# Talking-heads attention with a gated MLP: weight conversions and operand splits spread over three products, and another pool order

## The chip, the cores and the metric

The kernel runs on one core of one Trainium2 chip. The metric is the device time of one execution in microseconds (us). Of the five engines the text names PE (TensorE; PEld is its weight load, which runs beside its matmuls), DVE (VectorE), ACT (ScalarE), POOL (GpSimd) and SP (SyncE, here only a queue that issues transfers, in order). Each engine works through its own list of instructions in the order of that list, and an instruction that has to wait holds up those behind it.

## The reference

The reference computes attention in which the heads are mixed before and after the softmax, and then a gated MLP on its result, all in fp32:

```python
scores = scale * np.matmul(q, k.transpose(0, 1, 3, 2))        # q, k, v: 4 x 12 x 448 x 64
scores = np.einsum('bhij,hg->bgij', scores, w_pre)            # w_pre, w_post: 12 x 12
attn = np.exp(scores - np.max(scores, axis=-1, keepdims=True))
attn = attn / (np.sum(attn, axis=-1, keepdims=True) + 1e-09)
attn = np.einsum('bhij,hg->bgij', attn, w_post)
x = np.matmul(attn, v).transpose(0, 2, 1, 3).reshape(B * S, H * D)   # 1792 x 768
g = x @ w_gate                                                # w_gate, w_val: 768 x 1536
return (g * (1.0 / (1.0 + np.exp(-g))) * (x @ w_val)) @ w_out  # w_out: 1536 x 768
```

The weights of the MLP arrive as 64-bit floats, two 32-bit words each.

## The kernel before

**Attention** takes the first 400 us, batch after batch; the change leaves it as it is. It leaves X of the last two batches (896 tokens) in the on-chip memory as a high and a low part, and seven sums and blocks of X of the first two batches in device memory.

**Weights.** A weight is handled in 36 units of 128 x 768 elements: 12 of w_gate and 12 of w_val (indices 0 to 23, in turn), 12 of w_out (24 to 35). `load_raw` (L641) fetches the raw words; `convert` turns them into fp32 in seven operations: ACT's abs (L658), POOL's clamp (L660; on DVE for the first three units), and five on DVE (L662, L664, L668, L670, L672). `keep` (L675) stores the result to `w_d` in device memory, from where later products fetch it. A product with fp32 exactness takes each operand as a high part `hi`, made by ACT, and a low part `lo`, made by DVE as the difference, and issues hi*hi, lo*hi and hi*lo.

**Three products** follow on PE:

1. the gate and value products of the 896 tokens on chip: for each of 12 column blocks f four products of 18 matmuls (L810, L811, L814), upg and upv for two halves of 448 tokens. ACT takes the silu (L819), DVE the product with the value (L827). Units 0 to 23 are converted just before they are used, and split (`whi` L692, `wlo` L688). Beside that run the first w_out units, and `x_load` (L711) and `x_split` (L719 on ACT, L717 on DVE) of the seven X operands of the next product.
2. the same for the other 896 tokens as a Strassen-Winograd scheme: per f seven products of half size (`product`, L755, L756, L758), whose weights are combined (`w_sums`, L726 to L730) and split (L740 ACT, L737 DVE) first, and whose results are combined after (`combine`: copies a, b, c, d by ACT at L767, sums by DVE at L770, the silus sg0 and sg1 by ACT at L773, the products m0 and m1 by DVE at L780). Copy b frees the accumulator y for the seventh product. Results go to device memory or are summed (`a_sum`, L796, and `a_keep`, stores of L788). Six w_out units are converted beside it.
3. the product with w_out, again as seven terms of the same scheme (`AO`, index i), each of seven blocks c of 128 rows (`block`, 18 matmuls of L897, L898, L899). Each block needs a row tile `ar` (L876, and L872 where two are added), split into `ah` (L890, ACT) and `al` (L882, DVE); each term needs three units `o_b` (L857) or sums of them `ot` (`t_load` L845, `t_sum` L849), split into `ohi` (L867) and `olo` (L863). The first three row tiles of term 0 stand in an older tile, `a_first`.

**What sets the order.** Each step is registered with a number, `at_ff(n, fn)`, and the steps are issued in order of these numbers; one unit of n is about 1.1 us of the first product (48 products of 3.4 units in 184 us). `span` (163.2) is where the second product starts and `DOWN` where the third does. A unit that is wanted at n has d = n - 0.9, and these steps:

```python
d = n - LEAD
n1 = END + (d - 24.5) / 1.8                          # load_raw
for step, x in enumerate((17.2, 16.8, 12.9, 12.4, 11.9, 11.4, 10.9, 10.0)):
    at_ff(d - x, later(convert, u, step))            # 0: ACT, 1: POOL, 2 to 7: DVE
at_ff(d - 8.9, later(keep, u))
if u[0] != "o":
    at_ff(d - 3.8, later(split_w, b, u, False))      # whi, ACT
    at_ff(d - 2.8, later(split_w, b, u, True))       # wlo, DVE
```

**Pools.** At `DOWN` the pools of the second product on the right side of the on-chip memory (`t_p` temporaries, `mt` products, `xq` X operands, `ss` weight sums) are closed and those of the third take their place from the same end on, in the order in which they are opened: `ar` (six row tiles) first. A tile of a new pool waits for the last readers of what lay in its address range. `mag`, the tile of steps 0 to 7, has two buffers, and so unit k waits for L672 of the unit two before it in the order of conversions.

## Time and profile before

| | |
|---|---|
| median of 3 runs | 912.32 us |
| lowest and highest | 911.26 and 915.63 us |
| the profiled execution | 909.12 us |
| its span, first to last instruction | 907.4 us |
| mean granted clock of PE | 0.981 |
| busy: PE, PEld, DVE, ACT, POOL | 859.2, 705.9, 650.6, 457.8, 177.3 us |
| DMA | 218.03 MB, mean 240 GB/s |

Times in the trace count from the first instruction of the span. The granted clock is a share of PE's full 2.4 GHz. In waits, "A <- B" means that A stood idle until B had ended. Busy shares are averages over stages that have different limits, so the rows below are cut by stage.

### The profile page before, as it was taken

How to read it: one execution, taken by the hardware profiler on the slowest of the kernel's cores; microseconds unless marked ns; L12 is line 12 of the kernel's file. 1: busy time of each engine (PE TensorE's matmuls, PEld its weight loads, DVE VectorE, ACT ScalarE, POOL GpSimd, SP SyncE). 2: the span in 40 equal slices, each digit the busy share in tenths (PEclk: the TensorE clock that was granted, in tenths of full speed). 3: DMA queues.
4: the chain of work that ended last, by engine and by line, in shares of the span. 5: the costliest groups of instructions: out<-in, count | busy, mean ns of one | idle time of the engine just before them, and what ended most of it. 6: DMA issues, size and time to landing. Idle time of an engine off the chain costs nothing.

```text
span 907.4 us, 26549 instructions
## 1 busy us (share of the span) xinstructions
PE 859.2 (95%) x10886; PEld 705.9 (78%) x10886; DVE 650.6 (72%) x1204; ACT 457.8 (50%) x1042; POOL 177.3 (20%) x257
## 2 busy tenths in 40 slices
PE   8679999898999998989999999999999998999998
PEld 5355676566656666679889889999988998999998
DVE  4466576666756765667999898678988976855853
ACT  3376677666666767744333333255455454344321
POOL 2111111121211111124545543111111011002010
PEclk9698999999989999999999999999999999999999
DMA  9898988998898778536776865537776459968696
GB/s 215 291 323 260 289 284 243 335 305 284 266 321 266 261 232 299 186 108 208 261 254 213 280 224 194 169 105 219 224 224 208 144 199 332 348 212 195 169 303 158
DMA packets 187537, 218.03 MB, mean 240 GB/s; under 512 B 58360, under 2 KB 155160, under 8 KB 187416
## 3 DMA queue, kind: packets, MB, share of 16 engines
q1 hardware_dynamic: 181448, 207.97, 71.3%
q0 software_dynamic: 2080, 5.51, 3.5%
q10 hardware_dynamic: 3888, 2.86, 1.2%
q8 instruction: 86, 1.41, 0.6%
q14 instruction: 35, 0.29, 0.1%
HBM read 136.77 MB, written 79.54 MB: 238 GB/s over the span
## 4 chain that ended last, share of the span: by engine, by line
PE 69%; DVE 12%; DMA 8%; ACT 4%; issue 4%; SPq 2%; POOL 1%; ACTq 0%; DVEq 0%; POOLq 0%
PE pre L324 8%; PE av L410 8%; PE post L368 6%; PE p L755 5%; PE p L758 5%; PE p L756 5%; PE qk L275 5%; PE q L899 5%; PE q L898 5%; PE q L897 5%; DMA rs<-s_all 3%; PE upv L811 2%; PE upv L814 2%; PE upv L810 2%; DVE st L335 2%
## 5 line engine op out<-in xcount | busy, mean ns | idle before, releaser
L341 ACT ACTIVATE e<-pre,st 128x448 f32<-128x448 f32 x180 | 112.5, 630 | 89.6 <-DVE st L335 89.2
L660 POOL TENSOR_SCALAR mag<-mag 128x768 f32<-128x768 f32 x33 | 101.5, 3074 | 258.5 <-ACT mag L658 207.5
L335 DVE TENSOR_REDUCE st<-pre 128x1 f32<-128x448 f32 x180 | 104.3, 619 | 58.2 <-PE pre L324 55.3
L324 PE MATMUL pre<-rs,w_pre_blocks 64*64 64x448 f32 (+1 forms) x720 | 108.0, 573 | 17.7 <-DMA rs<-s_all 11.3
L368 PEld LDWEIGHTS post<-rw,e 60*64 60x64 f32 x5040 | 98.8, 137 | 31.6 <-issue 23.4
L352 POOL TENSOR_SCALAR rw<-w_post_gs,st 128x60 f32<-128x60 f32 x180 | 55.1, 320 | 322.1 <-DVE st L349 240.8
L368 PE MATMUL post<-rw,e 60*64 60x60 f32 x5040 | 105.1, 223 | 5.8 <-issue 4.1
L383 ACT ACTIVATE attnT<-post 128x420 f32<-128x420 f32 (+1 forms) x192 | 91.1, 542 | 22.2 <-PE post L368 21.5
L899 PE MATMUL q<-ohi,al 128*128 128x384 f32 x276 | 93.9, 340 | 2.3 <-DVE al L882 2.3
L897 PE MATMUL q<-ohi,ah 128*128 128x384 f32 x276 | 93.8, 340 | 1.6 <-ACT ah L890 1.6
L275 PE MATMUL qk<-kk,qt 64*64 64x448 f32 x672 | 93.8, 547 | 0.3 <-DVE w_post_gs L148 0.3
L898 PE MATMUL q<-olo,ah 128*128 128x384 f32 x276 | 93.4, 338 | 0.0
L410 PE MATMUL av<-attnT,vn 128*64 128x120 f32 (+9 forms) x1728 | 89.5, 263 | 3.3 <-DVE qt L252 1.8
L410 PEld LDWEIGHTS av<-attnT,vn 128*64 128x64 f32 (+1 forms) x1728 | 70.8, 136 | 16.0 <-issue 5.5
L284 DVE COPY stg<-qk 128x448 f32<-128x448 f32 x120 | 71.0, 617 | 8.3 <-PE qk L275 4.8
L890 ACT ACTIVATE ah<-ar 128x768 fp32r<-128x768 f32 x46 | 38.6, 844 | 58.4 <-PE q L898 28.8
L882 DVE TENSOR_TENSOR al<-ar,ah 128x768 fp32r<-128x768 f32 x46 | 43.8, 953 | 24.3 <-ACT ah L890 24.3
L275 PEld LDWEIGHTS qk<-kk,qt 64*64 64x64 f32 x672 | 32.3, 134 | 34.0 <-issue 22.3
L811 PE MATMUL upv<-x,wlo 128*128 128x448 f32 x144 | 53.2, 369 | 3.9 <-DVE wlo L688 3.7
L658 ACT ACTIVATE mag<-raw 128x768 f32<-128x768 f32 x36 | 32.8, 910 | 45.0 <-DVE w L672 25.4
L899 PEld LDWEIGHTS q<-ohi,al 128*128 128x128 f32 x276 | 52.3, 189 | 3.6 <-DVE al L882 3.6
L897 PEld LDWEIGHTS q<-ohi,ah 128*128 128x128 f32 x276 | 52.4, 190 | 2.5 <-ACT ah L890 2.5
(142 smaller groups left out, 1687.9 us busy)
## 6 DMA issues: line engine op xcount, KB each, us to landing
rs<-s_all SPq DMA_DIRECT2D x88, 448.0 KB, 5.5
s_all<-stg SPq DMA_DIRECT2D x60, 448.0 KB, 4.8
w_d<-w SPq DMA_DIRECT2D x36, 384.0 KB, 4.2
raw<-in_moe_w_gate_dram SPq DMA_DIRECT2D x12, 768.0 KB, 5.9
raw<-in_moe_w_val_dram SPq DMA_DIRECT2D x12, 768.0 KB, 7.4
raw<-in_moe_w_out_dram SPq DMA_DIRECT2D x12, 768.0 KB, 6.0
w<-w_d SPq DMA_DIRECT2D x24, 384.0 KB, 4.8
s_all<-stg SPq DMA_DIRECT2D x39, 224.0 KB, 5.0
```

Of the source, the lines that this page charges most:

```text
L275: nc.tensor.matmul(pt[x][i * HB:(i + 1) * HB], qt[b, c][hs, p, r:r + HB], kk[b, p][hs], start=True, stop=True)
L324: nc.tensor.matmul(pt[r][x * HB:(x + 1) * HB], wpre[i], xs[i, x], start=True, stop=True)
L335: nc.vector.tensor_reduce(sts[b, u][:, 0, r:r + 1], pts[b, t], axis=AX.X, op=ALU.max, negate=True)
L341: nc.scalar.activation(e, pts.pop((b, t)), AF.Exp, bias=st[:, 0, r:r + 1], scale=1.0, accum_out=st[:, 1, r:r + 1])
L368: nc.tensor.matmul(ats[b, u][y][o * HB:(o + 1) * HB, to, :m], et[b, t][i, c * P + x * HB:c * P + (x + 1) * HB], rw[b, t][i, :, :m], start= ...
L383: nc.scalar.activation(attnT[:part, i, n0:n1, y * HS:y * HS + m], pt[:part, n0:n1, :m], AF.Copy)
L410: nc.tensor.matmul(o, vn[b][part, h, c], a, start=(c == 0 and x == 0), stop=(c == NC - 1 and x == 2 - m))
L660: eng.tensor_scalar(mag, mag, f32_of(0x38000000), f32_of(0x47EFFFFF), op0=ALU.max, op1=ALU.min)
L811: nc.tensor.matmul(pt, lo[:, c], xh[:, c, ts], start=False, stop=False)
L897: nc.tensor.matmul(pt, ahi, bhi, start=f == 0, stop=False)
L898: nc.tensor.matmul(pt, ahi, blo, start=False, stop=False)
L899: nc.tensor.matmul(pt, alo, bhi, start=False, stop=f == NFH - 1)
```

## The change

It moves five things in the table of steps, and swaps pools:

- the seven X operands are loaded and split from n = 22 on in steps of 20, not from 14 in steps of 19;
- silu sg0 of the second product goes from 3.4 to 5.15, behind copy b at 5.05;
- the last `a_sum` goes from 8 steps of the last f to DOWN + 4 and DOWN + 6.5, the last `a_keep` from DOWN + 8 to DOWN + 11; `t_load` and `t_sum` go later by 4 to 12;
- three w_out units instead of four are converted in the first product, six in the second as before, and three instead of two in the third;
- raw load, ACT's abs and POOL's clamp come 1.6 sooner for every unit with d over 40;
- `bs` (the splits olo and ohi of odd terms) is opened ahead of `ar`.

```diff
-                n = 14.0 + 19.0 * i
+                n = 22.0 + 20.0 * i
...
-                    (1.05, "a"), (2.05, "c"), (3.1, "c11"), (3.4, "sg0"), (4.05, "d"), (5.05, "b"), (6.1, "c12"), (6.4, "sg1"),
+                    (1.05, "a"), (2.05, "c"), (3.1, "c11"), (5.15, "sg0"), (4.05, "d"), (5.05, "b"), (6.1, "c12"), (6.4, "sg1"),
...
-                    step(8.0, a_sum, f - NFH, 0)
-                    step(8.3, a_sum, f - NFH, 1)
-                    if f < NFC - 1:
-                        step(8.4, a_keep, f - NFH)
-                    else:
-                        at_ff(DOWN + 8.0, later(a_keep, f - NFH))
+                    last = f == NFC - 1
+                    for x, y, fn, *a in ((8.0, 4.0, a_sum, f - NFH, 0), (8.3, 6.5, a_sum, f - NFH, 1), (8.4, 11.0, a_keep, f - NFH)):
+                        at_ff(DOWN + y if last else n + x * T_P, later(fn, *a))
...
-                    at_ff(DOWN + (11, 11.5, 21, 22)[x] + 0.2 * j, later(t_load, bq, j))
-            for i, x in enumerate((20, 29, 33, 40)):
+                    at_ff(DOWN + (17, 17.5, 32, 33)[x] + 0.2 * j, later(t_load, bq, j))
+            for i, x in enumerate((24, 37, 41, 45)):
...
-            if ku < 4:
-                n = (2.75 + 2 * ku) * T_F[0]
-            elif ku < 10:
-                n = span + 10 + 22 * (ku - 4)
+            if ku < 3:
+                n = (2.75 + 3 * ku) * T_F[0]
+            elif ku < 9:
+                n = span + 12 + 23 * (ku - 3)
             else:
-                n = DOWN + 12 + 10 * (ku - 10)
+                n = DOWN + 12 + 9 * (ku - 9)
...
-                n1 = END + (d - 24.5) / 1.8
+                more = 1.6 if d > 40 else 0
+                n1 = END + (d - 24.5 - more) / 1.8
...
-                for step, x in enumerate((17.2, 16.8, 12.9, 12.4, 11.9, 11.4, 10.9, 10.0)):
+                for step, x in enumerate((17.2 + more, 16.8 + more, 12.9, 12.4, 11.9, 11.4, 10.9, 10.0)):
...
-    for name, bufs in (("ar", 6), ("ahl", 4), ("bw", 3), ("bs", 3), ("acc", 1), ("oo", 3)):
+    for name, bufs in (("bs", 3), ("ar", 6), ("ahl", 4), ("bw", 3), ("acc", 1), ("oo", 3)):
```

In the rows below a name is followed by unit or block numbers and last by the tile's own number.

**ACT, first product, before: from the mag of unit 11 on.** `mag` is step 0 of a unit's conversion, `whi_0_10` the high half of unit 10, `sg` a silu, `xw` the high half of an X operand.

```order
L658 ACTIVATE mag_11_8194<-raw_11_8122 128x768
L819 ACTIVATE sg_0_4_0_8219<-upg_0_4_0_8164 128x448
L719 ACTIVATE xw_1_8158<-xw_1_8158 128x1344
L819 ACTIVATE sg_0_4_1_8243<-upg_0_4_1_8200 128x448
L692 ACTIVATE whi_0_10_8251<-w_10_8129 128x768
L658 ACTIVATE mag_12_8254<-raw_12_8189 128x768
L692 ACTIVATE whi_0_11_8311<-w_11_8195 128x768
```

And now:

```order
L658 ACTIVATE mag_11_8177<-raw_11_8110 128x768
L692 ACTIVATE whi_0_9_8183<-w_9_8057 128x768
L819 ACTIVATE sg_0_4_0_8207<-upg_0_4_0_8153 128x448
L658 ACTIVATE mag_25_8210<-raw_25_8146 128x768
L819 ACTIVATE sg_0_4_1_8236<-upg_0_4_1_8188 128x448
L658 ACTIVATE mag_12_8239<-raw_12_8172 128x768
L692 ACTIVATE whi_0_10_8247<-w_10_8116 128x768
L658 ACTIVATE mag_13_8305<-raw_13_8234 128x768
L692 ACTIVATE whi_0_11_8311<-w_11_8178 128x768
```

The w_out unit 25 now stands here, and each mag stands ahead of the high half two units before it (mag_12, then whi_10), where it stood behind it.

**DVE, first product, before: from the low half of unit 8 on.** L662 to L672 are the conversion of a unit, `m_3` the gated product.

```order
L688 TENSOR_TENSOR wlo_0_8_8126<-w_8_8005,whi_0_8_8125 128x768
L662 TENSOR_SCALAR mag_25_8094<-mag_25_8094 128x768
L827 SCALAR_TENSOR_TENSOR m_3_8154<-sg_0_3_0_8091,upv_0_3_0_8099 128x448
L664 SCALAR_TENSOR_TENSOR mag_25_8094<-raw_25_8032,mag_25_8094 128x768
L668 TENSOR_SCALAR w_25_8095<-mag_25_8094 128x768
L670 SCALAR_TENSOR_TENSOR w_25_8095<-raw_25_8032,w_25_8095 128x768
L672 TENSOR_TENSOR w_25_8095<-mag_25_8094,w_25_8095 128x768
```

And now, from the low half of unit 10 on:

```order
L688 TENSOR_TENSOR wlo_0_10_8248<-w_10_8116,whi_0_10_8247 128x768
L662 TENSOR_SCALAR mag_25_8210<-mag_25_8210 128x768
L827 SCALAR_TENSOR_TENSOR m_4_8272<-sg_0_4_0_8207,upv_0_4_0_8215 128x448
L664 SCALAR_TENSOR_TENSOR mag_25_8210<-raw_25_8146,mag_25_8210 128x768
L668 TENSOR_SCALAR w_25_8211<-mag_25_8210 128x768
L670 SCALAR_TENSOR_TENSOR w_25_8211<-raw_25_8146,w_25_8211 128x768
L672 TENSOR_TENSOR w_25_8211<-mag_25_8210,w_25_8211 128x768
```

Unit 25 has gone from between the low halves 8 and 9 to between 10 and 11.

**SP at the start of the third product, before: from the last raw load to o_b21.** The brackets name the semaphores that a row waits for: DMAHW those of earlier transfers, the others those of engines.

```order
L641 DMA raw_35_10510<-in_moe_w_out_dram 128x2x768 [waits DMAHW3_49]
L876 DMA ar_0_3_10587<-a_n11_65 128x768 [waits DMAHW4_49,DMAHW5_49,DVE_49,PE_49]
L876 DMA ar_0_4_10589<-a_n11_65 128x768
L876 DMA ar_0_5_10595<-a_n11_65 128x768 [waits DMAHW6_49]
L675 DMA w_d_64<-w_34_10488 128x768 [waits DMAHW7_49,DVE_49]
L876 DMA ar_0_6_10622<-a_n11_65 128x768 [waits DMAHW0_49]
L857 DMA o_b21_0_10631<-w_d_64 128x768 [waits DMAHW1_49]
L857 DMA o_b21_1_10634<-w_d_64 128x768 [waits DMAHW2_49]
L857 DMA o_b21_2_10657<-w_d_64 128x768 [waits DMAHW3_49]
```

And now:

```order
L641 DMA raw_34_10478<-in_moe_w_out_dram 128x2x768 [waits DMAHW1_49]
L876 DMA ar_0_3_10575<-a_n11_65 128x768 [waits DMAHW2_49,PE_49]
L876 DMA ar_0_4_10577<-a_n11_65 128x768 [waits DMAHW3_49]
L876 DMA ar_0_5_10583<-a_n11_65 128x768 [waits DMAHW4_49]
L675 DMA w_d_64<-w_33_10461 128x768 [waits DMAHW5_49,DVE_49]
L641 DMA raw_35_10610<-in_moe_w_out_dram 128x2x768 [waits DMAHW6_49]
L876 DMA ar_0_6_10614<-a_n11_65 128x768 [waits DMAHW7_49]
L857 DMA o_b21_0_10620<-w_d_64 128x768 [waits DMAHW0_49]
L857 DMA o_b21_1_10623<-w_d_64 128x768 [waits DMAHW1_49]
L857 DMA o_b21_2_10647<-w_d_64 128x768 [waits DMAHW2_49]
```

ar_0_3 no longer waits for DVE; the PE event that it waits for is the end of the last product of the second stage, as before. The store of w_33 waits for DVE, and behind it stand now raw_35, ar_0_6 and o_b21_0.

**DVE at the start of the third product, before: from the end of unit 34's conversion to al_0_5.** `al_0_5` is the low half of row tile 5 of term 0, `olo_1_0` that of the first unit of term 1.

```order
L672 TENSOR_TENSOR w_34_10488<-mag_34_10487,w_34_10488 128x768
L796 TENSOR_TENSOR a_5_10437<-a_5_10437 128x896 x2
L882 TENSOR_TENSOR al_0_3_10625<-ar_0_3_10587,ah_0_3_10624 128x768
L882 TENSOR_TENSOR al_0_4_10662<-ar_0_4_10589,ah_0_4_10661 128x768
L662 TENSOR_SCALAR mag_35_10627<-mag_35_10627 128x768
L664 SCALAR_TENSOR_TENSOR mag_35_10627<-raw_35_10510,mag_35_10627 128x768
L863 TENSOR_TENSOR olo_1_0_10671<-o_b21_0_10631,ohi_1_0_10670 128x768
L668 TENSOR_SCALAR w_35_10628<-mag_35_10627 128x768
L670 SCALAR_TENSOR_TENSOR w_35_10628<-raw_35_10510,w_35_10628 128x768
L882 TENSOR_TENSOR al_0_5_10699<-ar_0_5_10595,ah_0_5_10698 128x768
```

And now:

```order
L672 TENSOR_TENSOR w_33_10461<-mag_33_10460,w_33_10461 128x768
L796 TENSOR_TENSOR a_5_10425<-a_5_10425 128x896
L882 TENSOR_TENSOR al_0_3_10617<-ar_0_3_10575,ah_0_3_10616 128x768
L796 TENSOR_TENSOR a_5_10425<-a_5_10425 128x896
L662 TENSOR_SCALAR mag_34_10586<-mag_34_10586 128x768
L664 SCALAR_TENSOR_TENSOR mag_34_10586<-raw_34_10478,mag_34_10586 128x768
L882 TENSOR_TENSOR al_0_4_10652<-ar_0_4_10577,ah_0_4_10651 128x768
L668 TENSOR_SCALAR w_34_10587<-mag_34_10586 128x768
L670 SCALAR_TENSOR_TENSOR w_34_10587<-raw_34_10478,w_34_10587 128x768
L863 TENSOR_TENSOR olo_1_0_10658<-o_b21_0_10620,ohi_1_0_10657 128x768
L672 TENSOR_TENSOR w_34_10587<-mag_34_10586,w_34_10587 128x768
L882 TENSOR_TENSOR al_0_5_10687<-ar_0_5_10583,ah_0_5_10686 128x768
```

The sums L796 have moved apart and al_0_3 between them; unit 34 is converted here, where before it was unit 35, and L672 of it stands between olo_1_0 and al_0_5.

## Rows read from the trace of the kernel before

**Rows 1.** Windows: busy us of PE, PEld, DVE, ACT, POOL, clock, DMA share, GB/s.

```profile
402.00:586.00 184.00, 179.92 (x1040) 163.87 (x1039) 157.49 (x197) 66.77 (x97) 81.22 (x26) 1.00 0.68 224
420.00:540.00 120.00, 116.15 (x565) 105.48 (x564) 114.19 (x135) 44.04 (x57) 61.15 (x20) 1.00 0.77 249
```

**Rows 2.** Waits from 400 us on: us in total, times, longest us.

```profile
ACT mag L658 <- DVE w L672: 25.4, 10, 3.9
...
ACT mag L658 <- DMA raw<-in_moe_w_gate_dram: 11.6, 5, 4.2
...
PEld upv L811 <- DVE wlo L688: 5.7, 5, 1.9
...
PEld p L755 <- ACT b L767: 1.8, 2, 1.2
```

**Rows 3.** DVE lines, 402 to 586 us: count, busy us, mean ns, idle before.

```profile
L664 DVE SCALAR_TENSOR_TENSOR mag<-raw,mag 128x768 uint32<-128x768 uint32 x26 | 27.0, 1040 | 0.5
L672 DVE TENSOR_TENSOR w<-mag,w 128x768 f32<-128x768 f32 x25 | 25.0, 1000 | 0.8
L670 DVE SCALAR_TENSOR_TENSOR w<-raw,w 128x768 f32<-128x768 uint32 x26 | 24.9, 958 | 0.9
...
L668 DVE TENSOR_SCALAR w<-mag 128x768 uint32<-128x768 uint32 x26 | 19.6, 753 | 0.7
L662 DVE TENSOR_SCALAR mag<-mag 128x768 uint32<-128x768 uint32 x26 | 15.0, 578 | 5.9 <-POOL mag L660 5.8
...
L717 DVE TENSOR_TENSOR xw<-xw 128x1344 fp32r<-128x1344 f32 x7 | 10.9, 1552 | 0.9 <-ACT xw L719 0.9
```

**Rows 4.** Timeline of ACT, second product: start, width, line, tiles, [idle before <- releaser].

```profile
660.11 0.58 ACT L773 ACTIVATE a<-a 128x448 f32<-128x448 f32 x1 [3.21 <-DVE a L770]
...
661.75 0.53 ACT L767 ACTIVATE b<-p 128x448 f32<-128x448 f32 x1
```

**Rows 5.** Timeline of PE, third product: block 0, 5's third matmul, 10 and 14.

```profile
742.46 0.33 PE L897 MATMUL q<-ohi,a_first 128*128 128x384 f32 x1
...
762.70 0.58 PE L899 MATMUL q<-ohi,al 128*128 128x384 f32 x1 [1.59 <-DVE al L882]
...
780.99 0.33 PE L897 MATMUL q<-ohi,ah 128*128 128x384 f32 x1
...
793.47 0.34 PE L897 MATMUL q<-ohi,ah 128*128 128x384 f32 x1
```

**Rows 6.** Window behind PE's longest wait there; columns as in rows 1.

```profile
763.00:766.30 3.30, 3.30 (x12) 3.30 (x12) 3.30 (x5) 1.12 (x3) 0.00 (x0) 0.51 1.15 360
```

**Rows 7.** Waits of SP's queue from 728 to 790 us.

```profile
SPq L876 <- DVE a L780: 17.2, 1, 17.2
```

**Rows 8.** Timeline of SP's queue at the start of the third product.

```profile
728.71 3.11 SPq L641 DMA_DIRECT2D raw<-in_moe_w_out_dram  x1
749.15 1.28 SPq L876 DMA_DIRECT2D ar<-a_n  x3
750.53 0.38 SPq L675 DMA_DIRECT2D w_d<-w  x1
...
751.42 0.56 SPq L857 DMA_DIRECT2D o_b<-w_d  x1
```

**Rows 9.** Timeline of ACT at the same place.

```profile
758.48 0.85 ACT L867 ACTIVATE ohi<-o_b 128x768 fp32r<-128x768 f32 x1 [3.50 <-DMA o_b<-w_d]
```

**Rows 10.** Timeline of POOL at the same place.

```profile
753.96 2.77 POOL L660 TENSOR_SCALAR mag<-mag 128x768 f32<-128x768 f32 x1 [13.73 <-ACT mag L658]
```

**Rows 11.** Timeline of DVE at the same place.

```profile
749.00 0.95 DVE L672 TENSOR_TENSOR w<-mag,w 128x768 f32<-128x768 f32 x1
...
755.02 0.96 DVE L882 TENSOR_TENSOR al<-ar,ah 128x768 fp32r<-128x768 f32 x1 [0.95 <-ACT ah L890]
...
759.36 0.96 DVE L863 TENSOR_TENSOR olo<-o_b,ohi 128x768 fp32r<-128x768 f32 x1 [1.04 <-ACT ohi L867]
...
761.70 0.95 DVE L882 TENSOR_TENSOR al<-ar,ah 128x768 fp32r<-128x768 f32 x1
```

## The prediction

> **What bounds the kernel now.** I read the windows by stage first, then the list of waits, then the timelines around the places at which TensorE (PE) waits. From 402 us on, the program is three matrix products, and in the window of the first one PE is busy 179.9 of 184 us at full clock [rows 1]: PE sets the time, and only its idle time can be won. There are three kinds of it.
>
> First product (402 to 586 us). The weight loads of upv stood idle five times, 5.7 us together, for VectorE's (DVE) low half of a weight, wlo [rows 2]. The reason is in the second window: between 420 and 540 us DVE is busy 114.2 of 120 us [rows 1]. It turns raw weights into fp32, and one unit costs it five operations of 0.58 + 1.04 + 0.75 + 0.96 + 1.00 = 4.3 us; a split of an X operand costs 1.55 us [rows 3].
>
> Second product (586 to 742 us). The weight loads of p waited 1.8 us in two waits for ScalarE's (ACT) copy b [rows 2]. Before one of them ACT stood 3.21 us in front of a silu whose sum DVE had not made, and copy b came behind it, at 661.75 [rows 4].
>
> Start of the third product. Its blocks of 18 matmuls run at (793.47 - 780.99) / 4 = 3.12 us once all is warm, but the first ten took 780.99 - 742.46 = 38.5 us, where ten such blocks take 31.2 [rows 5]: 7.3 us lost. The last and longest wait there is 1.59 us for al at 762.70 [rows 5], and behind it the granted clock was 0.51, the 1.2 GHz level, for 3.3 us [rows 6], worth 3.3 x 0.49 = 1.6 us. The chain behind it starts on SyncE's (SP) queue, which waited 17.2 us for DVE's products a [rows 7] and issued three ar loads at 749.15, w_34's store at 750.53 and o_b21's first load at 751.42 only [rows 8].
>
> What PE loses at these three places is 5.7 + 1.8 + 7.3 = 14.8 us, 1.6% of the run. That is all the change can win: it touches nothing before 402 us, and it adds and removes no instruction.
>
> **The change, part by part.** Three w_out units instead of four are converted in the first product, at wider spacing, and five instead of six X splits fall between 420 and 540 us. DVE's work in that window goes down by 4.3 + 1.55 = 5.9 us [rows 3], just what PE waited there (5.7). Demand and room were out by about that much, so I expect most of the wait to go, not all: between wlo_10 and wlo_11 DVE now has two whole units (25 and 12; its order shows unit 25 there), 8.7 us, in the time of two of PE's 48 products, 2 x 184 / 48 = 7.7 us, so its lead shrinks by a microsecond and more there, and again at unit 26. The order of ACT has a new wait too: mag_12 now stands ahead of whi_10, and mag_12 needs the buffer of mag_11, so DVE idles between w_11 and wlo_10 for two ACT operations of the size of a split, 0.85 us each [rows 9], 1.8 us with the hand-overs. It repeats at unit 26. The table places a wlo 3.7 of its steps ahead of the product that reads it, some 4 us, so a DVE that keeps time still has 2 us in hand, and PE loses nothing; if DVE lags there as it did, 2 x 1.8 = 3.6 us come back. Taken: 4.6 us won. Bounds: 5.7, and 0.
>
> Raw loads 1.6 units sooner: a raw load and its first two steps move together, so nothing is added. What is gained is time for POOL's clamp (2.77 us [rows 10]) ahead of DVE's next step. I count that within the 4.6.
>
> sg0 later: copy b no longer stands behind the silu that waits 3.21 us for DVE [rows 4]. The silu's reader comes 2 products later and has that much room. Taken: 1.4 of the 1.8 us; bounds 1.8 and 0.
>
> Pool order: `bs` takes the address range of the old temporaries, and `ar` that of the X operands. The order of SP shows what that does: the first ar load keeps its wait for PE and loses the one for DVE. PE's last product ends at 742.46 [rows 5], so three ar loads issue 749.15 - 742.7 = 6.4 us sooner [rows 8]. The stalls of blocks 3 and 4 go with that. But the next thing on SP is w_33's store, which waits for DVE's L672 as w_34's did, until 749.95 [rows 11]; then come raw_35 (new here) and ar_0_6, and then o_b21_0, at about 751.4 as before. I expect it to land as before, in time for ACT's ohi at 758.48 [rows 9]: ahead of it now stand a store, raw_35's load (twice an ar load's bytes) and one ar load, before it was four ar loads and a store. On DVE al_0_5 is queued behind olo_1_0, which waits for that ohi, and now also behind L672 of w_34. Before: olo at 759.36, al at 761.70 to 762.65 [rows 11]. After: olo 759.36, L672 0.9 us later, al from 761.1 to 762.05. Block 5 could start at 742.46 + 5 x 3.12 = 758.1 and needs al 0.35 us later: a stall of 762.05 - 758.4 = 3.6 us. **So most of what the earlier ar loads win is lost again at block 5**, and I keep the 1.6 us of half clock, because this idle time is longer than the 1.59 us before which it fell [rows 5, 6]. Lost after: 3.6 + 1.6 = 5.2 of 7.3; won: 2.1 us. Bounds: 5.5 won, if o_b21_0 lands 2 us sooner and the clock holds; 1.5 lost, if raw_35 holds SP for 3.11 us as raw_35 did once at 728.71 [rows 8].
>
> Later last sums, stores and t loads: the ot loads leave the crowd around 760 us, and ar_1_2 and ar_1_3 pass ahead of them. One more unit is converted after 742 us, 4.3 us of DVE's time, between splits that have 3 us a block. I cost it at nothing; without that cover it would be those 4.3 us.
>
> A rule weighed here: that unit's clamp on POOL now runs beside al_0_5 on DVE. The trace has that meeting: the clamp from 753.96 for 2.77 us [rows 10] and an al from 755.02, 0.96 us wide as anywhere [rows 11]. The Trainium skill (SBUF — State Buffer, "SBUF: two separate sides") says that GpSimd and a DVE operation with two SBUF inputs take a shared port pair as an exclusive lock, the loser blocked for a whole instruction. By that rule al_0_5 would wait for the clamp's end, up to 2.8 us more, and the sum below would be 5.3 in place of 8.1. The row shows no such block, so I keep 2.1.
>
> Sum: 4.6 + 1.4 + 2.1 = 8.1 us. The profiled execution took 909.12 us and would take 901.0. It lies 3.2 us below the median of the three runs shown (912.32), so the median to expect is 904.2.
>
> **Rivals.** (a) Everything goes but 2.8 us at block 5, because o_b21_0 lands a little sooner and the clock holds: 5.7 + 1.8 + 4.5 = 12 us, 900.3. For it: DVE's 5.9 us match the wait. Against it: the queue on SP. (b) Little moves: ACT's mag ahead of whi gives back 3.6 of the 5.7, and SP's raw_35 the gain at the joint: 2.1 + 1.4 - 0.5 = 3 us, 909.3, within 0.5%. ACT waited ten times, 25.4 us, for just this kind of buffer [rows 2]. (c) Slower: in the first product every whi now stands behind a mag that waits for its raw load; ACT waited 11.6 us in five waits for gate loads, up to 4.2 us [rows 2]. It decides once a mag comes more than some 3 us late, what a whi has in hand; at the longest wait, 4.2 - 3 = 1.2 us at each of the 12 gate units is 14 us, less the 3.5 won in the other two products: 10.5 us slower, 922.8. Against it: a raw load follows a store that is due about ten units of order before that whi is wanted. (d) POOL's clamp shuts DVE out while it runs beside al_0_5, 2.77 us [rows 10] longer at block 5: 8.1 - 2.8 = 5.3 us, 907.0. Against it stands the al of 0.96 us beside a clamp [rows 10, 11]. That the change does not do what it says is out for the pools: the order shows the wait gone.
>
> **How the numbers follow.** Half a per cent, 4.6 us, is about what a measurement of this kernel can tell from no change. Forecast 0.54; (a) 0.18; (b) 0.2; (c) 0.05; (d) 0.03. Faster by more than 0.5%, below 907.8: the forecast, (a) and (d), 0.75; within: 0.2; slower: 0.05. The range takes in (a) with another microsecond won at the joint (13 us, 899) and (b) with another microsecond lost (910.5).
>
> **What would show it.** Right: the upv waits for wlo under 1.5 us in total; no p wait for copy b; the first ar load of the third product issued near 743; PE's longest wait there at block 5, of 3 us or more, for al, behind an ohi that waits for o_b21. Wrong: upv waits above 3 us (ACT's order); a block-5 wait under 1 us (the loads land sooner than I think); new waits at blocks 9 to 14 (the extra unit, or ot loads that come too late).

## The result, and the profile after

The changed kernel takes 904.52 us (median of 8 runs, 902.01 to 907.0), the kernel before 912.79 beside it (8 runs, 908.45 to 915.63): a ratio of 0.9916, 95% interval [0.9889, 0.9944]. It is faster by 8.3 us; 8.1 was forecast, and the median expected was 904.2.

| | before | after |
|---|---|---|
| the profiled execution, its span | 909.12, 907.4 us | 903.57, 901.9 us |
| busy PE, PEld | 859.2, 705.9 us | 858.8, 706.9 us |
| busy DVE, ACT, POOL | 650.6, 457.8, 177.3 us | 647.6, 457.8, 177.0 us |
| mean granted clock of PE | 0.981 | 0.979 |
| last av matmul of attention ends | 412.02 us | 415.54 us |
| from there to the first p (first product) | 173.6 us | 168.4 us |
| from there to the first q (second product) | 156.8 us | 155.2 us |
| from there to the end of the last q (third product) | 161.4 us | 159.2 us |

The two profiled executions differ by 5.55 us only, since attention, whose instructions are the same, took 3.5 us longer in the one after. The three products lost 5.2 + 1.6 + 2.2 = 9.0 us. So I compare these three lengths from here on; they leave out what attention does from run to run.

The windows of after. In the stretch from 420 to 540 us VectorE is busy 109.4 us where it was 114.2, and PE 119.99 where it was 116.2 [rows 1]. Attention ends 3.5 us later here. Counted from its end the same stretch is the second row, and VectorE is busy 111.9 us in it. The third row is the stretch behind PE's waits in the third product: 1.2 GHz there, as in [rows 6], for 3.4 us.

```profile
420.00:540.00 120.00, 119.99 (x591) 110.56 (x591) 109.38 (x131) 43.24 (x57) 61.24 (x21) 1.00 0.76 247
423.54:543.54 120.00, 119.99 (x591) 110.58 (x590) 111.90 (x135) 42.92 (x56) 61.20 (x20) 1.00 0.77 246
759.00:762.41 3.41, 3.41 (x13) 3.41 (x12) 3.38 (x5) 2.45 (x4) 2.22 (x1) 0.50 1.12 338
```

The waits of after from 400 us on (us in total, times, longest). The wait of upv for wlo went from 5.7 to 0.8 us, the one of p for copy b [rows 2] is gone. VectorE now waits for whi, 5.1 us, which it had hardly done (0.3 us); PE hardly saw it.

```profile
ACT mag L658 <- DVE w L672: 31.0, 9, 5.5
...
DVE wlo L688 <- ACT whi L692: 5.1, 5, 1.7
...
PEld q L897 <- ACT ah L890: 1.9, 1, 1.9
PEld q L899 <- DVE al L882: 1.9, 3, 1.3
...
PEld upv L811 <- DVE wlo L688: 0.8, 2, 0.4
```

PE in the third product after: the first matmul, the two waits at block 5, and the starts of blocks 10 and 14. The first ten blocks take 775.57 - 739.16 = 36.4 us, where it was 38.5 [rows 5]; PE waits no more at blocks 3 and 9.

```profile
739.16 0.33 PE L897 MATMUL q<-ohi,a_first 128*128 128x384 f32 x1
...
757.02 0.44 PE L897 MATMUL q<-ohi,ah 128*128 128x384 f32 x1 [1.58 <-ACT ah L890]
...
758.64 0.45 PE L899 MATMUL q<-ohi,al 128*128 128x384 f32 x1 [1.01 <-DVE al L882]
...
775.57 0.33 PE L897 MATMUL q<-ohi,ah 128*128 128x384 f32 x1
...
788.05 0.34 PE L897 MATMUL q<-ohi,ah 128*128 128x384 f32 x1
```

SyncE's queue after. The ar loads start at 739.36, 0.2 us behind the last product's end (they were 6.7 us behind it [rows 5, 8]). Then w_33's store holds the queue until 747.16, and raw_35, ar_0_6 and o_b21 come behind it.

```profile
739.36 1.28 SPq L876 DMA_DIRECT2D ar<-a_n  x3
747.16 0.32 SPq L675 DMA_DIRECT2D w_d<-w  x1
747.53 0.44 SPq L641 DMA_DIRECT2D raw<-in_moe_w_out_dram  x1
748.01 0.51 SPq L876 DMA_DIRECT2D ar<-a_n  x1
748.56 1.52 SPq L857 DMA_DIRECT2D o_b<-w_d  x3
```

ACT after, at block 5: the ohi of o_b21_0 stands 8.14 us in front of its load, and the ah of row tile 5 is queued behind it.

```profile
755.01 0.84 ACT L867 ACTIVATE ohi<-o_b 128x768 fp32r<-128x768 f32 x1 [8.14 <-DMA o_b<-w_d]
...
756.13 0.83 ACT L890 ACTIVATE ah<-ar 128x768 fp32r<-128x768 f32 x1
```

VectorE after, at block 5: olo, L672 of unit 34, then al_0_5 (757.63 to 758.58), for which PE waits.

```profile
755.89 0.96 DVE L863 TENSOR_TENSOR olo<-o_b,ohi 128x768 fp32r<-128x768 f32 x1 [2.09 <-ACT ohi L867]
756.77 0.95 DVE L672 TENSOR_TENSOR w<-mag,w 128x768 f32<-128x768 f32 x1
757.63 0.95 DVE L882 TENSOR_TENSOR al<-ar,ah 128x768 fp32r<-128x768 f32 x1
758.53 1.55 DVE L863 TENSOR_TENSOR olo<-o_b,ohi 128x768 fp32r<-128x768 f32 x1
```

### The profile page after: what moved, and what is told of

The parts are those of the page before. It is cut to its first block, busy times and chain, and to the rows that moved or that the text cites. A ratio compares the mean times of both kernels' runs of the same rounds, so it can differ in the third digit from the quotient of the medians.

```text
span 901.9 us, 26545 instructions
## 1 busy us (share of the span) xinstructions
PE 858.8 (95%) x10886; PEld 706.9 (78%) x10886; DVE 647.6 (72%) x1204; ACT 457.8 (51%) x1042; POOL 177.0 (20%) x257
## 4 chain that ended last, share of the span: by engine, by line
PE 81%; DMA 6%; DVE 6%; ACT 3%; issue 2%; SPq 1%; POOL 0%; ACTq 0%; POOLq 0%; DVEq 0%
PE pre L324 8%; PE av L410 8%; PE post L368 7%; PE p L758 6%; PE p L755 6%; PE p L756 6%; PE q L899 5%; PE q L897 5%; PE q L898 5%; PE qk L275 5%; DMA rs<-s_all 4%; PE upv L811 3%; PE upv L810 3%; PE upv L814 3%; PE upg L814 3%; PE upg L810 3%
## 5 line engine op out<-in xcount | busy, mean ns | idle before, releaser
L324 PE MATMUL pre<-rs,w_pre_blocks 64*64 64x448 f32 (+1 forms) x720 | 110.1, 579 | 18.0 <-DMA rs<-s_all 13.6
L890 ACT ACTIVATE ah<-ar 128x768 fp32r<-128x768 f32 x46 | 38.6, 844 | 55.5 <-PE q L898 31.5
L324 PEld LDWEIGHTS pre<-rs,w_pre_blocks 64*64 64x64 f32 (+1 forms) x720 | 29.0, 138 | 33.2 <-issue 16.4
L810 PE MATMUL upv<-x,whi 128*128 128x448 f32 x144 | 52.8, 367 | 0.0
```

Source lines behind the costliest of these rows:

```text
L324: nc.tensor.matmul(pt[r][x * HB:(x + 1) * HB], wpre[i], xs[i, x], start=True, stop=True)
L810: nc.tensor.matmul(pt, hi[:, c], xh[:, c, ts], start=(c == 0), stop=False)
```

## The experiments

For the first product three theories stand against each other: **demand** (PE waited because VectorE had more to do than fits), **lead** (because raw words, abs and clamp came late) and **order** (because of where mag and whi stand on ACT). For the second product it is sg0's place. For the third it is the pool order, with what is left held up by **the queue** (o_b21 behind w_33's store), against late row tiles or VectorE itself.

All runs in one table, lengths in us as above. "Late" is what the matmul starts of the first product behind the last av matmul lie above the clean spacing (the sum over spacings of more than 0.22 us, less 0.203 each; one of 0.31 us at the start, which every trace has, is left out). It is steadier than the length: six traces with the very order of the changed kernel there give 0.3 to 0.7, though lengths of 168.4 to 170.0. "Idle" is the sum of PE's waits of more than 0.1 us in the third product. The ratio is to the kernel before on the same chip.

| kernel | first | late | second | third | idle | median | ratio and interval |
|---|---|---|---|---|---|---|---|
| before | 173.6 | 5.2 | 156.8 | 161.4 | 3.9 | 912.79 | |
| after | 168.4 | 0.5 | 155.2 | 159.2 | 2.6 | 904.52 | 0.9916 [0.9889, 0.9944] |
| units alone | 171.5 | 3.1 | 157.0 | 159.7 | 3.3 | 908.6 | 0.998 [0.9954, 1.0007] |
| raw step alone | 177.5 | 9.3 | 155.8 | 162.5 | 5.0 | 914.83 | 1.0041 [1.0018, 1.0065] |
| X, sg0, pools | 171.9 | 2.9 | 155.2 | 160.6 | 3.7 | 906.84 | 0.9943 [0.9913, 0.9972] |
| raw loads alone | 175.5 | 6.6 | 155.8 | 161.7 | 4.2 | 910.74 | 0.9997 [0.997, 1.0023] |
| after, no raw step | 167.8 | 0 | 155.3 | 162.2 | 3.7 | 900.66 | 0.9892 [0.9858, 0.9926] |
| after, old pools and sg0 | 168.4 | 0.5 | 156.3 | 163.2 | 5.3 | 907.73 | 0.9957 [0.9926, 0.9987] |
| after, o_b21 early | 170.0 | 0.3 | 155.2 | 157.7 | 2.5 | 898.8 | 0.9858 [0.9833, 0.9883] |
| and unit 34 later | 169.4 | 0.5 | 155.2 | 156.6 | 2.1 | 900.18 | 0.9885 [0.9861, 0.991] |
| and its clamp early | 170.0 | 0.3 | 155.2 | 155.1 | 0.4 | 899.7 | 0.9856 [0.9826, 0.9887] |
| and raw step in the third only | 167.8 | 0 | 155.2 | 154.5 | 0.3 | 897.52 | 0.984 [0.9804, 0.9876] |
| after, once more | 168.6 | 0.7 | 155.2 | 157.9 | 1.8 | 901.5 | 0.9872 [0.9839, 0.9905] |

**Units alone** on the kernel before: the `ku` table and the t loads and sums of the change, nothing else.

> The kernel before with the w_out table alone: three units instead of four in the first product, six in the second at the new places, three instead of two in the third, and the t loads and t sums later (they must follow the stores). Lengths of the three products in the trace, from the last av matmul to the first p, from there to the first q, from there to the last q: 173.6, 156.8, 161.4 us before and 168.4, 155.2, 159.2 with the whole change. Demand theory (one unit of 4.3 us taken out of the stretch in which VectorE is full): first product 169.3 to 170.5. Lead theory (what counts is that raw words, abs and clamp come sooner): first product within 1 us of 173.6. Order theory (the waits went because a mag now stands ahead of the whi two units before it): also within 1 us of 173.6. Second product unchanged at 156.8 by all three. Third: 160.5 to 162.5, since the first ar load still waits for VectorE.

Late fell from 5.2 to 3.1, the length by 2.1 us; expected were 3 to 4 by demand, under 1 by the other two. Demand explains the sign, but one unit less is worth half of what I took for it; a unit less and the wider spacing weren't tried apart. The second product is unchanged, as expected. The third is 1.7 us shorter, more than expected, though the first ar load still waits for VectorE there: PE's last wait at block 5 is 1.00 us in place of 1.59, and the granted clock stays at 1.00 behind it.

**The raw step alone** on the kernel before:

```diff
-                n1 = END + (d - 24.5) / 1.8
+                more = 1.6 if d > 40 else 0
+                n1 = END + (d - 24.5 - more) / 1.8
...
-                for step, x in enumerate((17.2, 16.8, 12.9, 12.4, 11.9, 11.4, 10.9, 10.0)):
+                for step, x in enumerate((17.2 + more, 16.8 + more, 12.9, 12.4, 11.9, 11.4, 10.9, 10.0)):
```

> The kernel before with raw load, abs and clamp 1.6 sooner and nothing else. Demand theory: VectorE has just as much to do between 420 and 540 us, so the first product stays at 172.5 to 174. Lead theory: 169 to 170. Order theory (mag ahead of whi is what comes with it): 169 to 170 too; if instead that order gives time back, as I feared, it is longer than 174.5. Second product 156 to 157.5, third 161 to 162.5.

It costs: late 9.3 for 5.2, the run 0.4% slower. The lead theory falls. Demand alone (172.5 to 174) does not cover 177.5 us either; the range that holds is that above 174.5, of an order on ACT that gives time back. Its waits in the first product:

```profile
ACT mag L658 <- DVE w L672: 34.7, 11, 5.5
...
PEld upv L811 <- DVE wlo L688: 8.2, 5, 2.7
...
DVE wlo L688 <- ACT whi L692: 5.4, 4, 1.7
```

VectorE waits 5.4 us for whi, where it waited 0.3: whi stands behind a mag that waits for L672 on VectorE itself.

**Raw loads alone** sooner on the kernel before, abs and clamp at their old places (the first hunk above without the second):

> The kernel before with the raw loads alone 1.6 sooner; abs and clamp stay where they were, so that ACT's order stays with whi ahead of mag. The raw step as a whole cost 3.9 us in the first product. If ACT's order is what costs (VectorE waits for whi behind a mag, 5.4 us in four): the waits for whi stay under 0.5 us and the first product is 172.5 to 174, as before. If it is the loads' place in the queue (other loads or stores held back): 176 to 178.

The waits for whi are 0.3 us in one, as ACT's order says, and late is 6.6, between 5.2 and 9.3. The length, 175.5, lies between what the two theories gave, so neither covers it: 2.7 of the 4.1 us come with mag and clamp, 1.4 with the loads. What the loads hold back wasn't tried further.

**X operands, sg0 and pools** on the kernel before, one part in each product (with the later last sums and stores):

```diff
-                n = 14.0 + 19.0 * i
+                n = 22.0 + 20.0 * i
...
-(3.4, "sg0")
+(5.15, "sg0")
...
-("ar", 6), ("ahl", 4), ("bw", 3), ("bs", 3), ("acc", 1)
+("bs", 3), ("ar", 6), ("ahl", 4), ("bw", 3), ("acc", 1)
```

> The kernel before with three parts that lie in three different products: X operands spaced out (first), sg0 at 5.15 (second), pool order with the later last sums and stores (third). Demand theory: one split of 1.55 us less in the full stretch, first product 172 to 172.6; lead theory: unchanged, 173.6. sg0 theory: second product 155.2 to 155.6 and no wait of p for copy b; if the waits went for another reason (fewer or later unit conversions), 156.8. Pool theory: first ar load within 1 us behind the last product, third product 158.5 to 160 with the longest wait at block 5; if the extra unit and the later t loads make the gain, 161 or more.

X operands: late 2.9 for 5.2, a gain of 2.3. It does not come from a split less in the full stretch: both traces have five X splits between 420 and 540 us (the sixth of the kernel before starts at 540.9), and in the 120 us counted from the end of attention VectorE is no less busy, 114.5 us (the row below; columns as in [rows 1]) for 114.2. The splits come 9 to 16 us later. PE's waits 30, 45 and 123 us behind attention shrink from 2.4 us together to 0.2, and the one 92 us behind it grows from 1.6 to 2.0.

```profile
422.02:542.02 120.00, 117.89 (x575) 107.32 (x574) 114.50 (x135) 44.31 (x57) 61.11 (x20) 1.00 0.76 249
```

sg0: all 1.6 us of the second product, and no wait for copy b. Pools: the third product is 0.9 us shorter, less than expected; the waits of block 3 are gone, and the one at block 5 is 2.40 us. A clamp of 8.18 us, for which VectorE waited 2.67 us, stands ahead of it and may be part of that (more below).

**The changed kernel without the raw step** (`more = 0`):

> The changed kernel with raw load, abs and clamp back at their old places. Only the first product should differ; as the mean pace of its matmuls differed by 1% between two traces of the same order, I read the sum of what the matmul starts there are late by (5.2 us before, 0.5 with the whole change, 3.1 with the units alone, 2.0 to 2.3 with the X operands alone, 8.2 of weight-load waits with the raw step alone). If the parts add up, units and X operands alone leave 5.2 - 2.1 - 3 = 0 to 1.5 us of it, no more than the whole change, and VectorE's waits for whi (5.1 us in five) are gone: the raw step is then of no use or a cost. If the raw step does its work only once VectorE has room (its waits for the clamp, 7.0 us in five with the units alone, are 3.0 in the whole change), 2 to 4 us of it come back here and the total is 906.5 to 908.

PE loses nothing in the first product: late 0, as the sum of the parts said (5.2 - 2.1 - 2.3 = 0.8). VectorE is busy 110.64 us from 420 to 540 (the window, columns as in [rows 1]), no less than in the changed kernel:

```profile
420.00:540.00 120.00, 120.00 (x594) 111.23 (x593) 110.64 (x134) 45.00 (x57) 60.73 (x21) 1.00 0.76 252
```

From the list of its waits: VectorE waits 1.2 us for whi instead of 5.1.

```profile
DVE wlo L688 <- ACT whi L692: 1.2, 2, 0.9
```

So it is the unit and the X operands that take the waits away, and the raw step is no help in the first product, neither alone nor in the whole. In the third product the first ten blocks take 34.2 us, for 36.4 and 35.1 in the changed kernel's two traces, but the whole loses more (one wait of 2.00 us at 774.64 for an al behind a t sum, and the half clock behind it); its median of 900.66 isn't told apart from 904.52 or 901.5.

**The changed kernel with the old pools and sg0 at 3.4:**

> The changed kernel with the pools in their old order and sg0 back at 3.4. Second product: 156.3 to 157 with waits for copy b if sg0's place was the cause, 155.2 if it was the fewer conversions there. Third product: with the old pools the first ar load waits again for VectorE's last products, and issues about 8 us behind the last product; block 3 waits for it, 161 to 163 in place of 159.2. If the pools are not the cause, 159 to 160.

sg0: 156.3 with waits of p for copy b, against 155.2. Of the 1.6 us, 1.1 hang on its place; the other 0.5 come with the rest of the change (sooner raw loads had taken 1.0 on the kernel before, 155.8 in both runs that have them). The wait in the list:

```profile
PEld p L755 <- ACT b L767: 1.4, 3, 0.6
```

Pools: the third product takes 163.2 us, 4.0 and 5.3 more than the two traces of the changed kernel. On SyncE's queue its first ar load issues at 744.35, 7.1 us behind the last product (737.2), and block 3 waits again.

```profile
744.35 1.28 SPq L876 DMA_DIRECT2D ar<-a_n  x3
```

**o_b21 early**, in the changed kernel:

```diff
-at_ff(n - 10.9 + 0.1 * j if i == 0 else n - 16 + j, later(b_load, i, j))
+at_ff(n - 10.9 + 0.1 * j if i == 0 else DOWN + 1.5 + 0.1 * j if i == 1 else n - 16 + j, later(b_load, i, j))
```

> The changed kernel with the three o_b21 loads ahead of w_33's store in SyncE's queue (step at DOWN + 1.5 instead of 16 ahead of term 1). Queue theory (block 5 waits because o_b21_0 stands behind a store that waits for VectorE): o_b21_0 issues at about 742.5 and lands before 749, ohi runs right behind the high half of row tile 4, the waits of 1.58 and 1.01 us and the stretch of half clock go, and the third product takes 154.5 to 156, 3 to 4.5 us less than 159.2: a total of 900.5 to 901.5 against 904.5. Rival, row tiles late: ar_0_5, or a later tile that o_b21 now stands ahead of, lands too late and PE waits 2 to 3 us at block 5 or 6 instead: 158.5 to 160. Rival, VectorE late: al_0_5 is held by the conversion of unit 34 alone, wait above 1 us, 157 to 159.

SyncE's queue has the three loads right behind the ar loads, and ACT's ohi runs at 746.50 instead of 755.01:

```profile
738.27 1.28 SPq L876 DMA_DIRECT2D ar<-a_n  x3
739.59 1.43 SPq L857 DMA_DIRECT2D o_b<-w_d  x3
746.07 0.32 SPq L675 DMA_DIRECT2D w_d<-w  x1
```

Block 5's waits went from 2.6 us (1.8 in the changed kernel's second trace, last in the table) to 1.30 and the half clock with them, but a wait stayed, as the rival "VectorE late" had it. The first ten blocks take 33.3 us, for 36.4 and 35.1 in the two traces of the changed kernel. VectorE's rows ahead of al_0_5 have no gap, and al_0_5 itself takes 1.58 us in place of 0.95 beside a clamp (the row of POOL):

```profile
750.30 0.95 DVE L882 TENSOR_TENSOR al<-ar,ah 128x768 fp32r<-128x768 f32 x1
751.17 0.55 DVE L668 TENSOR_SCALAR w<-mag 128x768 uint32<-128x768 uint32 x1
751.75 0.96 DVE L670 SCALAR_TENSOR_TENSOR w<-raw,w 128x768 f32<-128x768 uint32 x1
752.63 0.95 DVE L863 TENSOR_TENSOR olo<-o_b,ohi 128x768 fp32r<-128x768 f32 x1
753.50 0.95 DVE L672 TENSOR_TENSOR w<-mag,w 128x768 f32<-128x768 f32 x1
754.37 1.58 DVE L882 TENSOR_TENSOR al<-ar,ah 128x768 fp32r<-128x768 f32 x1
```

```profile
753.88 3.20 POOL L660 TENSOR_SCALAR mag<-mag 128x768 f32<-128x768 f32 x1 [11.02 <-ACT mag L658]
```

So the wait had two causes in a row: the queue first, and right behind it the conversion of unit 34, with 0.6 us of the 1.30 from the clamp. The third product, 157.7 us, missed the 154.5 to 156 of the queue theory; as a length it is hardly shorter than the 157.9 of the changed kernel's second trace, so the rows of block 5 and the ten blocks carry this reading. The median, 898.8, lies below the 900.5 to 901.5 expected.

**Unit 34 later** (35 and the first t sums too), with o_b21 early:

```diff
-                n = DOWN + 12 + 9 * (ku - 9)
+                n = DOWN + (12, 25, 32)[ku - 9]
...
-            for i, x in enumerate((24, 37, 41, 45)):
+            for i, x in enumerate((26, 37, 41, 45)):
```

> The changed kernel with o_b21 early (as in the run before) and unit 34 converted four steps later, unit 35 two, the first t sums two: now al_0_5 and al_0_6 stand ahead of, or between, the conversion's operations. If VectorE's fixed order was what still held block 5 (it had no idle time from 748.8 to 757 us with o_b21 early), the wait of 1.30 us there and that of 0.80 us for al behind a t sum that waits for its load go: third product 155 to 156.5 in place of 157.7, total 896.5 to 898. If the row tiles' landing in the crowd of transfers is the bound (DMA share 1.0 there), the waits only move to later blocks: 157.5 to 158.5.

The wait at block 5 and that behind the t sum are gone, and a new one of 1.73 us stands at block 6. Its cause I had not expected: the clamp of unit 34 took 9.89 us. The median, 900.18, missed the 896.5 to 898 expected.

```profile
743.81 9.89 POOL L660 TENSOR_SCALAR mag<-mag 128x768 f32<-128x768 f32 x1 [10.42 <-ACT mag L658]
754.05 2.87 POOL L660 TENSOR_SCALAR mag<-mag 128x768 f32<-128x768 f32 x1 [0.35 <-ACT mag L658]
```

VectorE in that time, from the first of nine two-operand operations without a gap to the last, and the conversion's next step, which waits for the clamp:

```profile
743.57 0.62 DVE L780 TENSOR_TENSOR a<-d,a 128x448 f32<-128x448 f32 x1
...
750.12 0.95 DVE L882 TENSOR_TENSOR al<-ar,ah 128x768 fp32r<-128x768 f32 x1
753.74 0.56 DVE L662 TENSOR_SCALAR mag<-mag 128x768 uint32<-128x768 uint32 x1 [2.67 <-POOL mag L660]
```

PE behind it:

```profile
759.26 0.44 PE L899 MATMUL q<-ohi,al 128*128 128x384 f32 x1 [1.73 <-DVE al L882]
```

The window that follows (columns as in [rows 1]) is at full clock, where the changed kernel had 0.50 behind its two waits:

```profile
759.30:762.50 3.20, 3.20 (x19) 3.20 (x20) 3.17 (x5) 0.17 (x1) 0.00 (x0) 1.00 0.85 282
```

**Its clamp early**: raw load, abs and clamp of unit 34 alone back to where they were, all else as in the run before.

```diff
-                n1 = END + (d - 24.5 - more) / 1.8
+                n1 = END + (d - 24.5 - more - (4.0 if u == ("o", 1, 4) else 0)) / 1.8
...
-                for step, x in enumerate((17.2 + more, 16.8 + more, 12.9, 12.4, 11.9, 11.4, 10.9, 10.0)):
+                ahead = 4.0 if u == ("o", 1, 4) else 0
+                for step, x in enumerate((17.2 + more + ahead, 16.8 + more + ahead, 12.9, 12.4, 11.9, 11.4, 10.9, 10.0)):
```

> The run with unit 34 later, and of that unit the raw load, abs and clamp back where they were (so that the clamp meets POOL about 4 us sooner, while VectorE works on the splits of the first row tiles); VectorE's order stays the same. With unit 34 later, its clamp took 9.89 us from 743.81, while VectorE ran two-operand sums and splits without a gap (743.6 to 751.1), and ended 2.63 us behind the last of them; VectorE then waited 2.67 us for it and PE 1.73 us at block 6. Lockout theory (a clamp that starts in an unbroken row of VectorE's two-operand operations gets nothing done until the row ends): here the clamp starts at about 740, as in the changed kernel, and takes 2.8 to 3.0 us; no wait of VectorE for it, PE's wait of 1.73 us gone, third product 154.7 to 155.8 in place of 156.6. Rival (the long span is only how the profile ends a POOL operation, and VectorE's wait came from elsewhere): span again above 5 us or wait again above 2 us, third product 156.2 to 156.8.

The clamp takes 2.89 us, VectorE goes through the same nine operations and then straight on to L662 at 751.95, and the idle time of the third product falls from 2.1 to 0.4 us. The early start takes the wait away.

```profile
740.48 2.89 POOL L660 TENSOR_SCALAR mag<-mag 128x768 f32<-128x768 f32 x1 [6.75 <-ACT mag L658]
```

**And the raw step in the third product only** (`more = 1.6 if d > DOWN else 0`):

> The run before with raw load, abs and clamp 1.6 sooner only for units of the third product, so that the first two products have the old places for them, as in the changed kernel without the raw step (excess over the clean pace 0 there, 0.5 us with the step). If the raw step is of no use in the first two products: first product 0.3 to 0.8 us shorter than in the run before, second the same (155.2 to 155.4), third the same within 0.3; total 0.5 us less, 895.5 to 897.5. If it is of use in the second (it took one wait for copy b away in the kernel before), second product 155.8 to 156.5.

Late 0, second product the same, third 154.5 with one wait of 0.3 us left for PE (0.6 for its weight loads, the row below). Two lengths miss: the first product is 2.2 us shorter than in the run before, where 0.3 to 0.8 was expected (0.3 of it is late, the rest pace, see the end), and the third 0.6 and not within 0.3. The three products take 477.6 us, 14.3 less than before; the forecast counted 14.8 us that could be won. Its median, 897.52, is the lowest of all; beside it on the same chip the changed kernel took 901.5. The runs of the two overlap, and so do those of the four kernels with o_b21 early, whose medians lie between 897.5 and 900.2. The lengths of the products differ by 4.1 us from the changed kernel's second trace.

```profile
PEld q L899 <- DVE al L882: 0.6, 1, 0.6
```

**The changed kernel once more:**

> The changed kernel once more, unchanged, beside the two versions above: 902 to 907 in total, first product 168.4 to 170, second 155.2, third 159 to 159.4 with waits at block 5 and half clock behind them, if what I read from its one trace repeats.

901.5 us, a little below the range given, and a third product of 157.9, 1.3 shorter than in the first trace. The waits at block 5 are the same two, for ah (0.77 us) and for al (1.00), with the half clock behind them.

## Why the prediction was right, and where not

The place of each gain holds: 8.3 us in the medians for 8.1, and by products 5.2, 1.6 and 2.2 for 4.6, 1.4 and 2.1. That the numbers agree to a few tenths is luck: measured once more, the changed kernel was 10.1 us faster than the kernel before beside it (901.5 for 911.63), and its products lost 5.0, 1.6 and 3.5.

**First product.** That the unit and the X operands cause the waits is shown, since with both changed nothing of them is left. For the X operands it is not VectorE's total work, as forecast: "five instead of six X splits" was misread (five before, five after), and with as much work in the stretch PE's matmuls are 2.3 us less late. Where the splits stand is what changed; how that gives 2.3 us stays open, as does whether the unit's 2.1 (of 4.3 forecast) come from less work or from wider places. VectorE's work in the stretch, counted from the end of attention, went down by 2.3 us and not 5.9, since PE goes through more products in it. That the sum comes near what was taken is in part luck. The wait of VectorE for whi behind a mag is there as priced (up to 1.7 us, 1.8 was taken), five times and not twice, and hidden by VectorE's lead as taken: PE sees two waits of 0.4 us. Rival (b) has its mechanism from this: without the lead, in the raw step alone, the same order costs.

**The step that failed** is "Raw loads 1.6 units sooner: [...] What is gained is time for POOL's clamp". It gains nothing in the first product: alone it makes PE 4.1 us later (1.4 of it with the loads, 2.7 with mag and clamp), in the whole 0.5 us. ACT goes by its list, so mag sooner is whi later: VectorE waits 5.4 us for whi with the raw step alone, 0.3 without it. I had named that cost one paragraph above and not set it against the gain.

**Second product.** Right: copy b no longer stands behind the silu. sg0's place alone gives all of it on the kernel before; in the whole change 1.1 us of it, since the rest of the change takes away part of the same waits.

**Third product.** The first ten blocks lose 36.4 - 31.2 = 5.2 us; 5.2 was forecast. Measured from the first q, olo starts at 16.7 us (16.9 forecast), al_0_5 ends at 19.4 (19.6), and the chain is the one named: w_33's store, o_b21_0, ohi, olo, al. The wait itself came in two pieces, 1.58 us for ah and 1.01 for al, 2.6 us and not 3.6: ah_0_5 is queued behind the same ohi on ACT, which I did not name. The half clock is there as taken, 3.4 us of it, worth 1.7. The rest of the 5.2 is 0.25 us in block 3 and the weight loads, which stop sooner than the matmuls: they wait 1.9 and 1.3 us, 0.6 more than 2.6.

"I cost it at nothing", of the extra unit, was wrong in a way that the total hides. Of its conversion the forecast counted L672 in front of al_0_5; as soon as the queue no longer held block 5, L668, L670 and L672 together did, with the clamp (1.30 us, the run with o_b21 early).

**Rival (d)** did not come about: al_0_5 started 0.2 us ahead of the clamp and took 0.95 us, and the olo behind it 1.55 us in place of 0.96. With o_b21 early, al_0_5 met the clamp and lost 0.63 us, not 2.77. A shut-out is in this kernel all the same, with POOL as the one that is shut out (below).

## What to carry to other kernels

Where an engine is nearly full, look at where work stands as well as at how much there is: here later places for the same splits were worth as much as a whole unit less. To start an input sooner on an engine that goes by its list pushes back what stands behind it, and that shows once there is no lead. When a wait is taken from the head of a queue, read on to the next waiting entry, and then to the next engine's fixed order: here a store, a conversion and a clamp stood one behind the other. The first ten blocks took 36.4 and 35.1 us in the two traces of the changed kernel, 33.3 with the first or the first two out of the way, and 31.5 and 31.3 with all three, where 31.2 is the clean pace.

## What the runs showed of the hardware

**A clamp on POOL and VectorE.** In all thirteen traces, each VectorE operation behind 400 us that ran 0.2 us or more above its usual width lay beside a clamp (22 in the kernel before, 17 after), no more than two to a clamp, most of them 0.5 to 0.63 us longer; a third to a half of the clamps had none. A clamp takes 2.77 us at the least. Of the 275 that took over 2.8 us, 204 ended 2.60 to 2.68 us behind the end of a VectorE operation, all five of over 4 us among them. Two of these five, 9.89 us (unit 34 later) and 8.18 us (X, sg0, pools), ended behind the last operation of an unbroken row of VectorE's, whose next instruction was the one that waits for the clamp. The other three took 4.2 us. The changed kernel has both cases at the same place. First trace, the clamp and the split beside it:

```profile
741.07 2.87 POOL L660 TENSOR_SCALAR mag<-mag 128x768 f32<-128x768 f32 x1 [6.76 <-ACT mag L658]
...
741.21 1.58 DVE L882 TENSOR_TENSOR a_first<-ar,a_first 128x768 fp32r<-128x768 f32 x1
```

Second trace (after, once more):

```profile
740.30 4.20 POOL L660 TENSOR_SCALAR mag<-mag 128x768 f32<-128x768 f32 x1 [6.77 <-ACT mag L658]
...
740.45 0.95 DVE L882 TENSOR_TENSOR a_first<-ar,a_first 128x768 fp32r<-128x768 f32 x1
```

My reading, argued and not shown: the clamp needs something of VectorE's once near its start and gets it where a VectorE operation ends, either at once, with the next operation 0.63 us longer, or only further on; then it runs freely. A gap of VectorE's is not needed: with its clamp early, unit 34's took 2.89 us in the middle of a row without one. What decides between the two is open. The Trainium skill (SBUF — State Buffer, "SBUF: two separate sides") says that whichever of the two starts first has the shared pair for its whole instruction and the other blocks fully. The two long clamps agree with that in so far as they got nowhere while VectorE went on; the others don't, since VectorE lost 0.6 us beside a clamp of 2.8 and not 2.8.

**The clock.** In the third product it fell to the 1.2 GHz level behind waits of 0.20 and 1.59 us close together (before), 1.58 and 1.01 (after), 0.77 and 1.00 (after, once more) and behind one of 2.00 (no raw step). It stayed at full behind 1.73 alone (unit 34 later) and 1.30 (o_b21 early). So the longest wait does not tell whether it falls: the forecast's reason for keeping the half clock, a wait longer than 1.59 us, would have failed for the 1.73.

**Pace.** With the same order and a granted clock of 1.00, the median spacing of the first product's matmuls was 0.202 or 0.203 us in four traces and 0.206 in two, and those two took 0.9 to 1.9 us longer over the 828 matmuls, late taken out. No row told why.
